# Three weight pieces under way instead of two, and a written order made again: attention with a top-128 expert layer on one core

## The chip, the core and the metric

The program runs on one core of a Trainium2 chip. The core has a matrix engine (TensorE, PE in the rows, with its weight loads as PEld), a vector engine (VectorE, DVE), a scalar engine (ScalarE, ACT), a general engine (GpSimd, POOL) and a sequencer that only issues transfers (SyncE, SP). Transfers of all queues are carried out by 16 DMA engines. The metric is the device time of one execution in microseconds (us); lower is better.

## The reference, cut to what matters

```python
# q, k, v: 8 batches x 12 heads x 448 tokens x 64
scores = cap * tanh(q @ k.T / sqrt(64) / cap)          # per head, 448 x 448
attn   = exp(scores - max) / (sum(exp(scores - max)) + 1e-9)
x      = (attn @ v), heads side by side                # 8 x 448 x 768
# expert layer, batch by batch
s      = x @ w_gate                                    # 448 scores
top    = the 128 tokens of the largest s
h      = relu(x[top] @ w1)                             # 128 x 1024
out    = x;  out[top] += sigmoid(s[top]) * (h @ w2)    # 128 x 768
```

## The kernel before, in words

Attention is cut into 24 *doubles* (three for each of 8 batches; a double is four heads), and each double into 7 *steps* of 64 key tokens, 168 steps in all. A step has one score product on TensorE (`ps`, line 450), a tanh and an exp on ScalarE (lines 501 and 504), one value product on TensorE that accumulates into `acc` (line 458), and a running sum of the exponentials on VectorE (`e`, line 554). Once per double VectorE turns the accumulator (`xT`, line 571), which frees the one PSUM accumulator for the next double; it turns and reduces the sums (lines 579 and 583), normalises (`xn` or `room`, line 674) and weighs the result for the token scores (lines 698 and 704).

After the third double of a batch comes its expert work. VectorE adds the token scores (`quads`, line 734); TensorE folds them (line 743); the score row goes out and comes back through HBM (`line`, `row`, lines 762 and 766) for every batch but the first; VectorE ranks every token (line 771) and builds the selection (`sel`, line 810); TensorE picks the indices (line 819); GpSimd gathers the 128 rows (`xe`, line 840). Then follow 36 matmuls with `w1` and 48 with `w2` per batch (line 961; each weight is held as a high and a low part, `w1h`, `w1l`, `w2h`, `w2l`), and GpSimd adds the result back with a scatter (line 1048; halves at line 1038 for the last batch). There are two `xe` buffers, so the selection of batch b can be written only when the scatter of batch b-2 has landed.

The weights come in 14 pieces of 128 rows, 6 of `w1` and 8 of `w2`. Of each piece GpSimd loads the high part (line 404), VectorE writes its negative into the low part (line 407, "cast"), and GpSimd loads the piece again and adds it into the low part (line 410). All 28 loads stand in GpSimd's queue in a fixed order, and a low load waits there for its cast.

The order of the work on all five engines is written by a planner before the program is built. It plays through the tasks with a duration for each, with a time for each transfer, and with a table `WAY` of eleven rows by 24 entries, which shifts priorities by double or stretch (`visit` and `enough`: how long TensorE stays at expert matmuls; `cast`: the 14 casts; and so on). The planner's own numbers set only this order; on the chip each engine runs its list in order and waits on semaphores for its operands.

Of the kernel before, what the change touches and what calls it, by code (L numbers as in the profile page):

```python
# [18 lines left out]
P = 128  # L19
# [21 lines left out]
ROWED = (1, 2, 3, 4, 5, 6, 7)  # L41
TURNED = (1, 2, 3, 4, 5), (1, 2, 3, 4)
WAY = {
    "visit": (14000, 8500, 14000, 4500, 7500, 7500, 1500, 7500, 5500, 2000, 2000, 1500, 6500, 3500,
        2500, 4500, 4000, 1500, 11000, 6000, 2500, 11000, 2500, 12500),
    "enough": (2, 3, 5, 5, 5, 5, 3, 1, 1, 3, 5, 3, 2, 2, 3, 5, 3, 2, 2, 5, 2, 5, 4, 1),
    "wait": (0, 1, 0, 0, 1, 1, 1, 1, 0, 0, 0, 0, 0, 0, 1, 0, 0, 0, 1, 1, 1, 1, 1, 0),
    "eager": (0, 2, 0, 2, 2, 0, 0, 0, 0, 0, 0, 0, 0, 0, 0, 0, 0, 0, 0, 0, 0, 0, 0, 0),
    "lag": (2, 2, 2.5, 3, 4, 2.5, 2.5, 4, 4, 2, 4, 4, 4, 2.5, 3, 4, 2.5, 2.5, 2.5, 3, 4, 4, 4, 4),
    "ask": (8, 0, -12, 12, 12, 0, -8, 8, 0, -4, -8, 8, 12, -8, -12, -8, -12, 8, -4, 12, 4, -8, -12,  # L50
        0),
    "fin": (14, 14, -4, -4, -8, -8, 0, -4, 8, 0, -4, -8, -8, 8, -8, 4, 0, -4, -4, -4, 14, 4, 8, 14),
    "turn": (20, 20, 0, 20, 20, 28, 10, 20, 20, 20, 28, 0, 0, 0, 0, 0, 0, -10, -10, 10, 10, 10, 20,
        20),
    "reserve": (30000, 30000, 0, 10000, 80000, 38000, 70000, 10000, 70000, 46000, 0, 0, 46000,
        70000, 70000, 46000, 20000, 20000, 30000, 46000, 30000, 46000, 46000, 0),
    "sums": (0, 8, 0, 0, 0, -2, 0, -2, -2, -2, -2, 8, -4, 0, -4, 0, 0, 0, 0, 0, 2, 8, 8, 0),
    "cast": (0, -20, 0, 10, 10, 10, 10, 10, 20, 10, 10, 10, 10, 10, 20, 20, 20, 0, -30, 20, -10,
        -10, 10, -30),
}  # L60


# [22 lines left out]
class Plan:  # L85
# [6 lines left out]
    def add(self, *a, **k):  # L92
        t = Task(*a, **k)
        t.n = len(self.tasks)
        self.tasks.append(t)
        return t
# [288 lines left out]
def w_tile(K, shape, dt, tag, i, name):  # L385
    return K.work.tile(shape, dt, tag=f"{tag}{i}", name=name, bufs=1)


def weights(tc, K, w1, w2, first=None, lv=None):
    nc = tc.nc  # L390
    parts = [(nm, w, i, m) for nm, w, n, m in (("w1", w1, K.ND, K.F), ("w2", w2, K.NF, K.DM))
             for i in range(n)]
    K.weights = {"w1": [], "w2": []}
    def pace(t):
        nc.gpsimd.tensor_copy(K.pace, first.v[0:1, 0, 0, 0:1])

    paced = K.plan.add("POOL", 120, pace, [lv], prio=-30) if lv else None
    before = [paced, paced]
    for n, (nm, w, i, m) in enumerate(parts):
        hi, lo = K.wts[nm + "h"][:, i, :], K.wts[nm + "l"][:, i, :]  # L400
        rows = w[i * P:(i + 1) * P, :]

        def high(t, hi=hi, rows=rows):
            nc.gpsimd.dma_start(hi, rows)

        def less(t, hi=hi, lo=lo):
            nc.vector.tensor_scalar(lo, hi.bitcast(F32), -1.0, None, op0=ALU.mult)

        def low(t, lo=lo, rows=rows):
            nc.gpsimd.dma_start(lo, rows, accum_op=ALU.add)  # L410

        h = K.plan.add("POOL", 950, high, before[:1], prio=3 * n, load=(1, P * m * 4), lat=1200)
        v = K.plan.add("DVE", 0.56 * m, less, [h], prio=6 + 3 * n, seg=("cast", n, 1))
        l = K.plan.add("POOL", 950, low, [v], prio=6 + 3 * n, load=(1, P * m * 5), lat=2000)
        before = [before[1], l]
        K.weights[nm].append(l)


# [295 lines left out]
def add_two(nc, out, two, both, n):  # L714
    if both is not None:
        nc.vector.tensor_reduce(out, both[:, :, :n].rearrange("p r c -> p c r"), axis=AX.X, op=ALU.add)
        return
    nc.vector.tensor_copy(out, two[0][:, :n])
    nc.vector.tensor_tensor(out, out, two[1][:, :n], op=ALU.add)


def select_tasks(tc, K, b):
    nc = tc.nc
    add, S, NCH, DM, NG = K.plan.add, K.S, K.NCH, K.DM, K.NG
    NB = S // Q
    vals = K.vals[b % 2]
    score = vals[:, 1, :]
    p0 = (b + 1) * NG * K.NS + 5
    ask = ("ask", (b + 1) * NG - 1, 1)
    box = {}  # L730

    def total(t):
        part, quads = K.part[b], K.quads[b % 2]
        nc.vector.tensor_tensor(quads[:, :NB], part[:, 0, :], part[:, 1, :], op=ALU.add)
        for g in range(2, NG):
            nc.vector.tensor_tensor(quads[:, :NB], quads[:, :NB], part[:, g, :], op=ALU.add)

    def fold(t):
        box["pc"], box["all"] = K.two(t)
        for i in range(2):  # L740
            for r in range(2):
                for m in range(2):
                    nc.tensor.matmul(box["pc"][r][HALF[m], :NCH], lhsT=K.fold[HALF[r], i, :],
                                     rhs=K.quads[b % 2][HALF[r], 2 * m + i::4], start=(i == 0),
                                     stop=(i == 1))

    def by_token(t):
        add_two(nc, score, box["pc"], box["all"], NCH)

    def rows(t):  # L750
        box["pr"] = K.two(t)[0][0]
        for c in range(NCH):
            nc.tensor.transpose(box["pr"][:, c * P:(c + 1) * P],
                                score[:, c:c + 1].to_broadcast([P, P]), K.ident)

    def row_copy(t):
        box["row"] = w_tile(K, [P, P * NCH], F32, "row", t.got["row"], "row")
        nc.vector.tensor_copy(box["row"].rearrange("p (q c) -> p c q", c=NCH),
                              box["pr"].rearrange("p (c q) -> p c q", c=NCH))

    def out_scores(t):
        nc.sync.dma_start(K.line[b % 2].rearrange("(p c) -> p c", c=NCH), score)

    def in_row(t):
        box["row"] = w_tile(K, [P, P * NCH], F32, "row", t.got["row"], "row")
        nc.sync.dma_start(box["row"], K.line[b % 2].partition_broadcast(P))

    def rank(t, c):
        m = min(P, S - c * P)
        jk = w_tile(K, [P, P, NCH], BF16, "jk", 0, "jk")  # L770
        nc.vector.scalar_tensor_tensor(  # L771
            out=jk[:m], in0=box["row"][:m].rearrange("p (q c) -> p q c", c=NCH),
            scalar=score[:m, c:c + 1], in1=K.least[:m, :, NCH - 1 - c:2 * NCH - 1 - c],
            op0=ALU.subtract, op1=ALU.is_ge, accum_out=K.rk[:m, c:c + 1])

    to = add("DVE", 340, total, K.scored[b], prio=p0, seg=ask)
    where = "S" if b else "X"
    fo = add("PE", 230, fold, [to], prio=-50, take=(where,), mode="att", late=True)
    bt = add("DVE", 70 if b else 330, by_token, [fo, *K.picked.get(b - 2, ())], prio=p0, seg=ask,
             give=[(where, fo)])  # L780
    if b in ROWED:
        ro = add("SP", 0, out_scores, [bt], prio=p0 - 30, load=(1, P * NCH * 4), lat=1200)
        landed = add("NONE", 0, lambda t: None, [ro], prio=-100)
        rc = add("SP", 0, in_row, [landed], prio=p0 - 30, take=("row", "rk"), load=(1, P * S * 4), lat=1500)
    else:
        ro = add("PE", 450, rows, [bt], prio=p0, take=(where,), mode="full")
        rc = add("DVE", 1030, row_copy, [ro], prio=p0, seg=ask, take=("row", "rk"),
                 give=[(where, ro)])
    count = [add("DVE", 680, lambda t, c=c: rank(t, c), [rc], prio=p0 + 1, seg=ask)
             for c in range(NCH)]  # L790
    add("NONE", 0, lambda t: None, count, prio=-100, give=[("row", rc)])
    final, hot = None, []
    for s0 in range(0, K.C, P):
        oh, final = expert_tasks(tc, K, b, s0, min(P, K.C - s0), count, final, vals, p0)
        hot.append(oh)
    add("NONE", 0, lambda t: None, hot, prio=-100, give=[("rk", rc)])
# [314 lines left out]
def end_batch(tc, K, D):  # L1111
    if D.grp < K.NG - 1:
        return
    b = D.b
    select_tasks(tc, K, b)
    K.plan.add("NONE", 0, lambda t: None, [*K.stores[b], *K.scored[b]], prio=-100,
               give=[("xn", K.first_n[b])])
# [92 lines left out]
def slow_path(tc, K, w1, w2):  # L1210
    K.plan = Plan(SIZES)
    K.fast_now = False
    K.last_heavy = [None, None]
    K.xn, K.part, K.xn_slot, K.first_n, K.stores, K.scored, K.picked = {}, {}, {}, {}, {}, {}, {}
    K.weighed = {}
    load_consts(tc, K)
    load_gate(tc, K)
    weights(tc, K, w1, w2)
    K.plan.run_in_order()
    general_path(tc, K)  # L1220
# [68 lines left out]
```

## Time and profile before

| | us |
|---|---|
| median of 3 runs | 443.87 (442.96 to 444.3) |
| the profiled execution | 443.99 |
| its span, first to last instruction | 442.2 |
| TensorE busy | 425.6 (96%) |
| VectorE busy | 370.6 (84%) |
| ScalarE busy | 347.2 (79%) |
| GpSimd busy | 49.1 (11%) |

The span is read in stretches: up to about 62 us only attention of the first batch is there; then expert matmuls come between the attention steps; the last score product stands near 374 us, and after it come mostly expert matmuls. A busy TensorE is not TensorE at its peak, since matmuls overlap in the array and their ends are modelled; so distances between starts are used as prices.

### The profile page before, as it was taken

How to read it: one execution, taken by the hardware profiler on the slowest of the kernel's cores; microseconds unless marked ns; L12 is line 12 of the kernel's file. 1: busy time of each engine (PE TensorE's matmuls, PEld its weight loads, DVE VectorE, ACT ScalarE, POOL GpSimd, SP SyncE). 2: the span in 40 equal slices, each digit the busy share in tenths (PEclk: the TensorE clock that was granted, in tenths of full speed). 3: DMA queues.
4: the chain of work that ended last, by engine and by line, in shares of the span. 5: the costliest groups of instructions: out<-in, count | busy, mean ns of one | idle time of the engine just before them, and what ended most of it. 6: DMA issues, size and time to landing. Idle time of an engine off the chain costs nothing. (4 is left out here: it accounts for less than half of the span.)

```text
span 442.2 us, 9958 instructions
## 1 busy us (share of the span) xinstructions
PE 425.6 (96%) x4106; PEld 233.1 (53%) x4106; DVE 370.6 (84%) x515; ACT 347.2 (79%) x403; POOL 49.1 (11%) x56
## 2 busy tenths in 40 slices
PE   8999899899999999999999999999999999999994
PEld 2242233344444548447554445644459539597984
DVE  3579999999999998999988999999997799853111
ACT  6999999999999993898859998899996598131320
POOL 5023110402101002000100000001002001002011
PEclk9999999899999999999999999999999999999998
DMA  7699996699935954792666943566782750552121
GB/s 241 238 249 249 320 274 185 183 254 261 217 132 151 224 125 110 207 308 65 161 168 181 223 144 110 139 168 152 252 207 64 178 152 1 109 115 36 37 36 42
DMA packets 58839, 73.72 MB, mean 167 GB/s; under 512 B 19266, under 2 KB 43202, under 8 KB 58786
## 3 DMA queue, kind: packets, MB, share of 16 engines
q1 hardware_dynamic: 52546, 53.67, 42.4%
q0 software_dynamic: 5808, 18.88, 19.7%
q8 instruction: 34, 0.56, 0.5%
q10 hardware_dynamic: 432, 0.46, 0.4%
q14 instruction: 19, 0.16, 0.1%
HBM read 54.76 MB, written 18.23 MB: 165 GB/s over the span
## 5 line engine op out<-in xcount | busy, mean ns | idle before, releaser
L501 ACT ACTIVATE p<-ps,sc 128x896 f32<-128x896 f32 (+1 forms) x169 | 164.8, 1014 | 15.2 <-PE ps L450 14.9
L504 ACT ACTIVATE p<-p,capc 128x896 f32<-128x896 f32 x168 | 171.0, 1060 | 0.4
L450 PE MATMUL ps<-qk 64*64 64x448 f32 x1288 | 148.0, 545 | 2.7 <-ACT p L501 2.6
L458 PE MATMUL acc<-p,v 64*64 64x448 f32 x1288 | 147.7, 545 | 2.3 <-DVE xT L571 1.1
L554 DVE TENSOR_TENSOR e<-e,p 128x896 f32<-128x896 f32 x119 | 128.2, 1078 | 8.3 <-ACT p L504 6.7
L450 PEld LDWEIGHTS ps<-qk 64*64 64x64 f32 x1288 | 44.6, 132 | 76.3 <-ACT p L501 40.3
L458 PEld LDWEIGHTS acc<-p,v 64*64 64x64 f32 x1288 | 46.5, 134 | 67.7 <-issue 49.3
L1048 POOL DMA_INDIRECT out<-xe,idx x7 | 12.7, 1809 | 216.1 <-ACT xe L1030 182.1
L987 ACT ACTIVATE hs<-pb 128x512 f32<-128x512 f32 x16 | 9.6, 600 | 31.8 <-PE pb L961 31.8
L961 PE MATMUL pb<-w2h,hh 128*128 128x384 f32 x128 | 28.4, 343 | 0.0
L571 DVE STREAM_TRANSPOSE xT<-acc 128x896 f32<-128x896 f32 x24 | 26.4, 1098 | 2.3 <-PE acc L458 2.3
L554 DVE TENSOR_TENSOR e<-p 128x896 f32<-128x896 f32 x24 | 25.8, 1075 | 2.9 <-ACT p L504 2.9
L961 PE MATMUL pb<-w2h,hl 128*128 128x384 f32 x128 | 28.2, 338 | 0.0
L961 PE MATMUL pb<-w2l,hh 128*128 128x384 f32 x128 | 28.2, 338 | 0.0
L771 DVE SCALAR_TENSOR_TENSOR jk<-row,vals,least 128x512 bf16<-128x512 f32 (+1 forms) x32 | 23.9, 746 | 3.7 <-DMA row<-line 2.9
L961 PE MATMUL pb<-w1h,xh 128*128 128x512 f32 x96 | 26.0, 399 | 0.0
L704 DVE TENSOR_REDUCE part<-jk 128x14 f32<-128x896 f32 x24 | 25.8, 1074 | 0.1
L579 DVE STREAM_TRANSPOSE turned<-e 128x896 f32<-128x896 f32 x23 | 25.3, 1100 | 0.3
L961 PE MATMUL pb<-w1l,xh 128*128 128x512 f32 x96 | 25.3, 395 | 0.0
L961 PEld LDWEIGHTS pb<-w2h,hh 128*128 128x128 f32 x128 | 22.2, 188 | 5.9 <-issue 4.9
L961 PE MATMUL pb<-w1h,xl 128*128 128x512 f32 x96 | 25.0, 394 | 0.0
L583 DVE TENSOR_REDUCE T<-turned 128x28 f32<-128x896 f32 x23 | 24.6, 1069 | 0.1
(106 smaller groups left out, 360.3 us busy)
## 6 DMA issues: line engine op xcount, KB each, us to landing
qk<-in_qk SPq DMA_DIRECT2D x46, 448.0 KB, 5.2
v<-in_v SPq DMA_DIRECT2D x23, 448.0 KB, 5.1
out<-xn SPq DMA_DIRECT2D x16, 224.0 KB, 4.4
out<-room SPq DMA_DIRECT2D x16, 224.0 KB, 3.9
w1h<-in_moe_w POOLq DMA_DIRECT2D x6, 512.0 KB, 8.4
w1l<-in_moe_w POOLq DMA_DIRECT2D x6, 512.0 KB, 8.1
w2h<-in_moe_w POOLq DMA_DIRECT2D x8, 384.0 KB, 8.9
w2l<-in_moe_w POOLq DMA_DIRECT2D x8, 384.0 KB, 7.2
```

The costliest lines, as they stand in the source:

```text
L450: tc.nc.tensor.matmul(ps[HALF[r], j, c0:c1], lhsT=D.qk[r][HALF[j], at:at + HD], rhs=D.qk[r][HALF[j], 2 * HD + c0:2 * HD + c1], start=True, ...
L458: tc.nc.tensor.matmul(D.acc[HALF[j], r, :K.S], lhsT=D.v[HALF[r], s, j, :], rhs=D.P[s][HALF[r], j, :], start=(s == 0), stop=(s == K.NS - 1))
L501: nc.scalar.activation(D.P[s][:, :, c0:c1], box[c0][:, :, c0:c1], AF.Tanh, scale=K.sc)
L504: nc.scalar.activation(D.P[s], D.P[s], AF.Exp, scale=K.cap)
L554: nc.vector.tensor_tensor(box["E"], box["E"] if n else D.P[s0], D.P[s], op=ALU.add)
L571: nc.vector.transpose(D.xT, D.acc[:, :, :S])
L579: nc.vector.transpose(box["turned"], parts[0]())
L583: nc.vector.tensor_reduce(box["T"], box["turned"].rearrange("p j (b k) -> p j b k", k=Q), axis=AX.X, op=ALU.add)
L704: nc.vector.tensor_reduce(K.part[b][:, grp, :], box["jk"], axis=AX.X, op=ALU.add)
L771: nc.vector.scalar_tensor_tensor(out=jk[:m], in0=box["row"][:m].rearrange("p (q c) -> p q c", c=NCH), scalar=score[:m, c:c + 1], in1=K.lea ...
L961: nc.tensor.matmul(X["acc" + n_ops][:M, :ns[1]], lhsT=X[l][:, i, :M], rhs=K.wts[r][:, i, ns[2]], start=bool(start and n == 0), stop=(stop ...
L1048: nc.gpsimd.indirect_dma_start(out=K.out[b], out_offset=bass.IndirectOffsetOnAxis(ap=X["idx"][:M], axis=0), in_=X["xe"][:M], in_offset=Non ...
```

## The change

Three things change. In `weights`, the high load of a piece is made to follow the low load of the piece three before it, where it was two before. In the planner's transfer times, a high load is counted 2500 ns later than its bytes in place of 1200, a low load 3000 in place of 2000, the score row's way out 3000 in place of 1200 and its way back 2500 in place of 1500. And the table `WAY` is another one, so that the order on every engine is written anew. The instructions are the same ones, and as many of each.

```diff
-    "visit": (14000, 8500, 14000, 4500, 7500, 7500, 1500, 7500, 5500, 2000, 2000, 1500, 6500, 3500,
...
+    "visit": (8000, 1500, 4500, 2000, 3500, 1500, 6000, 12500, 7000, 5500, 5500, 4500, 11000, 2000,
...
-    before = [paced, paced]
+    before = [paced] * 3
...
-        h = K.plan.add("POOL", 950, high, before[:1], prio=3 * n, load=(1, P * m * 4), lat=1200)
+        h = K.plan.add("POOL", 950, high, before[:1], prio=3 * n, load=(1, P * m * 4), lat=2500)
         v = K.plan.add("DVE", 0.56 * m, less, [h], prio=6 + 3 * n, seg=("cast", n, 1))
-        l = K.plan.add("POOL", 950, low, [v], prio=6 + 3 * n, load=(1, P * m * 5), lat=2000)
-        before = [before[1], l]
+        l = K.plan.add("POOL", 950, low, [v], prio=6 + 3 * n, load=(1, P * m * 5), lat=3000)
+        before = [*before[1:], l]
...
-        ro = add("SP", 0, out_scores, [bt], prio=p0 - 30, load=(1, P * NCH * 4), lat=1200)
+        ro = add("SP", 0, out_scores, [bt], prio=p0 - 30, load=(1, P * NCH * 4), lat=3000)
         landed = add("NONE", 0, lambda t: None, [ro], prio=-100)
-        rc = add("SP", 0, in_row, [landed], prio=p0 - 30, take=("row", "rk"), load=(1, P * S * 4), lat=1500)
+        rc = add("SP", 0, in_row, [landed], prio=p0 - 30, take=("row", "rk"), load=(1, P * S * 4), lat=2500)
```

The lines of the changed kernel are one lower than those before (404 is 403 there). On GpSimd's queue, the loads of the first pieces before, in their order:

```order
17 L404 DMA w1h<-in_moe_w 128x1024 x2
18 L410 DMA w1l<-in_moe_w 128x1024
19 L404 DMA w1h<-in_moe_w 128x1024
20 L410 DMA w1l<-in_moe_w 128x1024
21 L404 DMA w1h<-in_moe_w 128x1024
22 L410 DMA w1l<-in_moe_w 128x1024
23 L404 DMA w1h<-in_moe_w 128x1024
```

The same queue after the change, from the first load on:

```order
17 L403 DMA w1h<-in_moe_w 128x1024 x3
18 L409 DMA w1l<-in_moe_w 128x1024 x2
19 L403 DMA w1h<-in_moe_w 128x1024
20 L409 DMA w1l<-in_moe_w 128x1024
21 L403 DMA w1h<-in_moe_w 128x1024 x2
22 L409 DMA w1l<-in_moe_w 128x1024
23 L403 DMA w2h<-in_moe_w 128x768
```

Three high loads go out ahead of the first low load, where there were two; the gather of batch 0 (line 840, 839 after) has 18 of the 28 weight loads ahead of it before and 24 after.

On TensorE, the last `w2` matmuls of batch 0 before stand behind the fold of batch 1 (`quads_118`), the pick of batch 1 and the fold of batch 2 (`quads_117`), with 82 score products and 77 value products ahead of them:

```order
148 L743 MATMUL two<-quads_117,fold 64x4 x8
149 L450 MATMUL ps<-qk 64x448 x8
150 L458 MATMUL acc<-p,v 64x448 x4
151 L961 MATMUL pb<-w2h,hh 128x384 x4
152 L961 MATMUL pb<-w2l,hh 128x384 x4
153 L961 MATMUL pb<-w2h,hl 128x384 x4
154 L961 MATMUL pb<-w2h,hh 128x384 x4
155 L961 MATMUL pb<-w2l,hh 128x384 x4
156 L961 MATMUL pb<-w2h,hl 128x384 x4
157 L961 MATMUL pb<-w1h,xh 128x512 x6
```

After the change they stand next to the fold of batch 1, with 63 score products and 58 value products ahead:

```order
109 L742 MATMUL two<-quads_118,fold 64x4 x8
110 L457 MATMUL acc<-p,v 64x448 x4
111 L449 MATMUL ps<-qk 64x448 x4
112 L457 MATMUL acc<-p,v 64x448 x4
113 L600 MATMUL two<-T,same 64x14 x4
114 L960 MATMUL pb<-w2h,hh 128x384 x4
115 L960 MATMUL pb<-w2l,hh 128x384 x4
116 L960 MATMUL pb<-w2h,hl 128x384 x4
```

The whole expert work of batch 0 has moved ahead by 19 steps of attention, and the `w1` matmuls of batch 1 that followed it directly now come 22 score products after it.

Near the end of TensorE's list, the pick of the last batch (`vals_112`) before stands among the `w1` matmuls of batch 6:

```order
434 L961 MATMUL pb<-w1h,xh 128x512 x4
435 L867 MATMUL pb<-ident,hs 128x128 x4
436 L961 MATMUL pb<-w1h,xh 128x512 x2
437 L961 MATMUL pb<-w1l,xh 128x512 x3
438 L819 MATMUL two<-vals_112,sel 64x2 x16
439 L961 MATMUL pb<-w1l,xh 128x512 x3
440 L961 MATMUL pb<-w1h,xl 128x512 x6
```

After the change it stands here:

```order
422 L866 MATMUL pb<-ident,hs 128x128 x4
423 L960 MATMUL pb<-w1h,xh 128x512 x2
424 L960 MATMUL pb<-w1l,xh 128x512 x6
425 L960 MATMUL pb<-w1h,xl 128x512 x4
426 L818 MATMUL two<-vals_112,sel 64x2 x16
427 L960 MATMUL pb<-w1h,xl 128x512 x2
428 L960 MATMUL pb<-w2h,hh 128x384 x4
```

It is seven `w1` matmuls later; the matmuls around it are the same.

## Rows read from the trace of the kernel before

**Rows 1.** The page, busy time (share of the span) and instructions of three engines.
```profile
PE 425.6 (96%) x4106; PEld 233.1 (53%) x4106; DVE 370.6 (84%) x515; ACT 347.2 (79%) x403; POOL 49.1 (11%) x56
```

**Rows 2.** Windows: stretch, length, busy time of each engine, clock, DMA share, GB/s.
```profile
62.00:188.00 126.00, 121.72 (x1246) 59.94 (x1242) 122.62 (x174) 111.89 (x130) 15.84 (x16) 0.99 0.73 190
188.00:374.00 186.00, 184.82 (x1797) 102.66 (x1794) 174.50 (x223) 164.47 (x187) 8.76 (x6) 1.00 0.59 159
374.00:437.00 63.00, 61.01 (x437) 51.18 (x435) 25.16 (x49) 13.03 (x24) 7.72 (x6) 1.00 0.33 62
```

**Rows 3.** Waits of VectorE from 62 to 188 us: total, times, longest.
```profile
DVE sel L810 <- DMA out<-xe,idx: 1.7, 1, 1.7
DVE rec L615 <- PE two L601: 0.8, 2, 0.5
```

**Rows 4.** Timeline of VectorE: start, duration, instruction, [idle before, releaser].
```profile
62.35 1.11 DVE L571 STREAM_TRANSPOSE xT<-acc 128x896 f32<-128x896 f32 x1
63.38 1.05 DVE L554 TENSOR_TENSOR e<-e,p 128x896 f32<-128x896 f32 x1
...
175.49 0.69 DVE L810 SCALAR_TENSOR_TENSOR sel<-iota,rk 128x512 f32<-128x512 f32 x1 [1.68 <-DMA out<-xe,idx]
...
187.74 1.11 DVE L571 STREAM_TRANSPOSE xT<-acc 128x896 f32<-128x896 f32 x1
...
202.03 1.07 DVE L571 STREAM_TRANSPOSE xT<-acc 128x896 f32<-128x896 f32 x1
```

**Rows 5.** Timeline of TensorE: the last expert matmuls of batch 0, first of batch 1.
```profile
167.06 0.86 PE L961 MATMUL pb<-w2h,hl 128*128 128x384 f32 x4
167.76 1.54 PE L961 MATMUL pb<-w1h,xh 128*128 128x512 f32 x6
169.13 1.53 PE L961 MATMUL pb<-w1l,xh 128*128 128x512 f32 x6
```

**Rows 6.** Timeline of TensorE: attention, first value products of doubles 13 and 14.
```profile
186.61 0.93 PE L458 MATMUL acc<-p,v 64*64 64x448 f32 x8
187.36 0.93 PE L450 MATMUL ps<-qk 64*64 64x448 f32 x8
...
188.90 0.98 PE L458 MATMUL acc<-p,v 64*64 64x448 f32 x8
...
208.94 1.71 PE L458 MATMUL acc<-p,v 64*64 64x448 f32 x16
```

**Rows 7.** Timeline of GpSimd: weight loads, and the scatter of batch 0.
```profile
42.55 0.87 POOL L404 DMA_DIRECT2D w2h<-in_moe_w  x1
...
53.34 0.86 POOL L404 DMA_DIRECT2D w2h<-in_moe_w  x1
...
115.43 0.88 POOL L410 DMA_DIRECT2D w2l<-in_moe_w  x1 [4.18 <-DVE w2l L407]
...
168.82 2.40 POOL L1048 DMA_INDIRECT out<-xe,idx  x1 [34.02 <-DMA row<-line]
```

**Rows 8.** Timeline of TensorE: the pick of the last batch.
```profile
406.55 0.64 PE L819 MATMUL two<-vals,sel 64*64 64x2 f32 x32 [0.94 <-DVE sel L810]
```

**Rows 9.** Waits of TensorE from 188 us to the end: total, times, longest.
```profile
PE two L819 <- DVE sel L810: 1.4, 2, 0.9
PE two L601 <- ACT p L501: 0.5, 1, 0.5
PE two L601 <- DVE T L583: 0.4, 1, 0.4
PE acc L458 <- DVE xT L571: 0.4, 1, 0.4
```

**Rows 10.** DMA issues from 44 to 66 us: size each, median us to landing.
```profile
w2h<-in_moe_w POOLq DMA_DIRECT2D x2, 384.0 KB, 10.4
w2l<-in_moe_w POOLq DMA_DIRECT2D x2, 384.0 KB, 9.0
w1l<-in_moe_w POOLq DMA_DIRECT2D x1, 512.0 KB, 8.3
```

**Rows 11.** Windows as in Rows 2, early stretches.
```profile
9.00:24.00 15.00, 14.59 (x188) 4.62 (x184) 6.93 (x8) 15.00 (x17) 4.09 (x6) 1.00 0.70 237
24.00:44.00 20.00, 19.38 (x252) 7.18 (x248) 19.16 (x28) 20.00 (x23) 4.30 (x7) 1.00 1.01 262
44.00:66.00 22.00, 19.46 (x208) 6.58 (x204) 21.86 (x29) 21.41 (x24) 3.31 (x5) 1.00 1.08 296
66.00:88.00 22.00, 19.48 (x212) 6.90 (x210) 21.74 (x36) 20.31 (x24) 5.79 (x7) 0.92 0.64 188
```

**Rows 12.** Timeline of TensorE: its longest wait.
```profile
80.14 1.64 PE L450 MATMUL ps<-qk 64*64 64x448 f32 x8 [1.77 <-ACT p L501]
```

More of the change, by code (lines that the diff above doesn't have):

```diff
@@ L43 @@
 WAY = {
-    "visit": (14000, 8500, 14000, 4500, 7500, 7500, 1500, 7500, 5500, 2000, 2000, 1500, 6500, 3500,
[L45 to L56, printed above, removed]
@@ L57 @@
-    "sums": (0, 8, 0, 0, 0, -2, 0, -2, -2, -2, -2, 8, -4, 0, -4, 0, 0, 0, 0, 0, 2, 8, 8, 0),
-    "cast": (0, -20, 0, 10, 10, 10, 10, 10, 20, 10, 10, 10, 10, 10, 20, 20, 20, 0, -30, 20, -10,
-        -10, 10, -30),
+    "visit": (8000, 1500, 4500, 2000, 3500, 1500, 6000, 12500, 7000, 5500, 5500, 4500, 11000, 2000,
+        8000, 6000, 3000, 14000, 14000, 14000, 8500, 4000, 6500, 5500),
+    "enough": (5, 3, 2, 5, 2, 3, 1, 3, 4, 2, 4, 4, 4, 1, 4, 1, 1, 1, 1, 5, 1, 4, 1, 1),
+    "wait": (1, 1, 0, 1, 1, 1, 0, 0, 1, 1, 1, 0, 0, 1, 0, 1, 0, 1, 1, 0, 1, 0, 0, 1),
@@ new lines @@
+    "eager": (0, 2, 2, 2, 2, 0, 0, 0, 1, 1, 2, 0, 0, 0, 0, 0, 0, 0, 0, 0, 0, 0, 0, 0),
+    "lag": (1, 1, 1.5, 2, 2, 2.5, 2.5, 4, 4, 4, 4, 4, 2, 4, 2, 2, 4, 4, 4, 4, 4, 4, 4, 4),
+    "ask": (12, -12, 0, 12, 0, 12, 8, 8, 8, -4, 0, 12, 12, -12, -12, -4, -4, 8, 8, 8, 4, 4, 4, 4),
+    "fin": (-8, 0, 4, 8, -8, 4, -8, 14, 8, -4, 0, -4, 8, 4, -8, -8, 4, 0, 0, -8, 14, -4, 14, 4),
+    "turn": (20, 10, -10, 28, 28, 28, -10, 20, 0, 0, 0, 20, 10, 10, 0, 28, 20, 28, 10, 20, -10, 10,
+        28, 28),
+    "reserve": (20000, 50000, 50000, 50000, 50000, 20000, 20000, 20000, 50000, 30000, 54000, 42000,
+        30000, 0, 80000, 54000, 30000, 0, 20000, 38000, 30000, 20000, 20000, 10000),
@@ L60 @@
+    "sums": (8, -4, 2, 2, 2, 2, 2, 0, -2, -2, -2, -2, -2, 8, 4, -2, 0, 0, 0, 0, 0, -2, 0, 8),
+    "cast": (10, 20, 10, 20, 20, 20, 20, 20, 10, -30, -20, -30, -30, -20, -30, -20, -30, 20, -20,
+        -20, 0, -20, -10, 0),
 }
```

## The prediction, on record before the result was known

> **What bounds the kernel now.** I read the page's busy times first [rows 1], then the windows by stretch [rows 2], then the waits, then the timelines. The page says TensorE, at 96%, but that share is an average over stretches, so I asked the windows which engine has no room left in each. From 62 to 188 us VectorE works 122.6 of 126.0 us, and nearly all that is missing are two kinds of waits: 1.7 us for the selection of batch 2, which stands until the scatter of batch 0 has landed, and 0.8 us for sums of TensorE [rows 2, 3]. TensorE in the same stretch is shown busy 121.7 us, but its parts are stretched: four matmuls of attention (eight records) take 0.75 us from start to start [rows 6], which makes 1.5 us for a step, and VectorE needs more than that for a step and its share of the rest. The place where the one hands the time to the other is the accumulator: at 187.74 us VectorE starts to turn the accumulator of double 12, and the first value product of double 13 starts at 188.90, 1.16 us later, which is the 1.11 us of the turn and its signal [rows 4, 6]. So up to 188 us the pace is VectorE's. From 188 to 374 us TensorE works 184.8 of 186.0 us, and after 374 us 61.0 of 63.0 [rows 2]; there the pace is TensorE's, and whatever does not shorten its list or its waits is worth nothing.
>
> **The change part by part.** No instruction is added or removed, so only idle time on the pacing engine can come or go. I counted both written orders up to the same point, the turn of double 12 and the first value product of double 13.
>
> Ahead of that value product TensorE has in both kernels the same list: 700 score and value matmuls (175 products of four), 72 of `w1`, 48 of `w2`, three picks, three folds. Ahead of that turn VectorE has in both 137 large operations of about 1.0 us (62.35 to 63.38 for one [rows 4]), 12 rankings, 14 casts, three selections and the same expert splits; after the change one reciprocal more, which I count at 0.3 us. Equal lists end at a different time only through waits. VectorE's early part is also the same: ahead of the turn that starts at 62.35 us there are 38 large operations in both, and one cast more after, so there is no head start.
>
> The 1.7 us wait goes. Before, the last `w2` matmuls of batch 0 end at 167.8 us, just before the first `w1` matmuls of batch 1, its scatter is issued at 168.82, and the selection of batch 2 starts at 175.49 [rows 4, 5, 7]. After the change those `w2` matmuls stand 19 steps of attention earlier; 38 products of 0.75 us are 28.6 us. The scatter's landing then comes near 147 us and cannot be what the selection of batch 2 waits for. The 0.8 us for sums I leave, since nothing shows it gone. First term: 1.7 - 0.3 = 1.4 us earlier at the first value product of double 13. Bounds: at the good end all 2.5 us of [rows 3] go; at the bad end the early casts cost VectorE waits of their own (the rival below), so this term reaches from -2.5 to +4.4.
>
> Does the 1.4 us last? For double 14, VectorE has 5.2 us more ahead of its turn than before (four large operations and one `xt`), while TensorE's list is the same again. Before, the product came 208.94 - 202.03 - 1.11 = 5.8 us after the turn was done [rows 4, 6]. The turn is now 5.2 later in VectorE's list, and 1.4 us of lead are common to both, so 0.6 us of cover stay, and with it the lead. If that cover were short by a microsecond, the lead would shrink by as much.
>
> From there TensorE's list holds the same instructions in both kernels, and the count of changes between attention and expert matmuls is 27 in both, so I move nothing there, except one wait that I can see. The pick of the last batch stands 0.94 us for its selection [rows 8], which itself waits for the scatter of batch 5. In the new order seven more `w1` matmuls stand ahead of it; six take 1.37 us (167.76 to 169.13 [rows 5]), so seven take 1.6 us, more than the wait. Second term: 0.9 us. The other waits of TensorE in this part, 2.7 - 0.9 = 1.8 us in all [rows 9], are the bound below; above, one new wait of the longest kind seen, 1.77 us [rows 12].
>
> The planner's longer transfer times change only the order. The score rows' way is one of them: its ranking is not a wait in [rows 3], so I give it nothing.
>
> Three pieces under way: the casts of the last pieces move up in VectorE's list by some 24 us of its work, so the last low load, at 115.43 us before [rows 7], would go out near 91 us. TensorE first needs `w2` near 110 us in the new order, and all of it near 124, so with landings of 9 to 10 us [rows 10] TensorE does not wait for weights. VectorE might: a cast waits in line for its high load and holds back everything behind it, sums and turns included. I followed GpSimd's list against the casts: the shortest time from issue to cast is about 10 us, for the second piece of `w2`, issued near 44.5 and cast near 54.5. Before, the pair at 42.55 and 53.34 us had 11 to 12 us, and landings took 10.4 us [rows 7, 10]. It is close; but by 51 us the new order has put out no more than one transfer beyond the old one, and that one early, between 9 and 24 us, where the DMA engines are busy 0.70 of the time [rows 11]. I take zero, and price the failure below.
>
> One rule speaks against the third piece. From 24 to 66 us the DMA engines are busy 1.01 and 1.08 of the time [rows 11]. The Trainium skill (DMA: Bandwidth & Descriptors, Issuing engines are not separate DMA queues) says that transfers of all queues run on the same 16 engines and interleave. By it a third piece in that stretch only lengthens every landing, the pieces come no sooner, and the waits go to VectorE. The same page (Anatomy of one DMA, SWDGE path) puts one such load at 2.0 us plus its bytes over 436 GB/s, an estimate of 2.9 us for 384 KB; the rows show 10.4 us under this load, so the measured number decides, and by the page's number the first rule's rival would fall away.
>
> **Sum.** 443.99 (profiled execution; span 442.2 and 1.8 around it) - 1.4 - 0.9 = 441.7 us. That execution is 0.12 us above the median of 443.87, which I neglect. What this kernel's measurement can tell from no change is about 0.3%, 1.3 us, so "faster" begins at 442.5.
>
> **Rivals.** *Slower: casts wait for late loads.* Place: VectorE between 50 and 90 us, where its time is the kernel's. By 56 us the new order has three transfers more under way than the old. From 44 to 66 us the DMA engines were already full, so each costs its place in line, and I price one at 1.5 us (384 KB at the 296 GB/s of [rows 11], 1.3 us, and something for the second read of the adding load): 4.4 us. Then 441.7 + 4.4 = 446.1 us. It decides as soon as the second `w2` piece takes over 10.0 us to land; for it speak the 10.4 of [rows 10], against it the nearly equal number of transfers by 51 us.
>
> *No change: the lead is given back.* The lead of 1.4 us reaches the stretch paced by TensorE, and the new places of expert work bring as many new waits (a pick, a sum or a turn that is late by a microsecond, as in [rows 9]). A wait there may cost twice: around the 1.77 us wait [rows 12] the granted clock is 0.92 over 22 us [rows 11], which is some 1.8 us at the lower of its two levels. Before, VectorE's pace hid that; after 188 us nothing would. Result 443.5 to 444.3, 443.9.
>
> *Faster by more.* The other waits of 1.8 us and 0.8 us go too: 441.7 - 2.6 = 439.1 us. For it: the planner now counts transfers nearer to what the rows show. Against it: those waits have nothing to do with transfers.
>
> **Chances.** Forecast 0.42 (its own range 440.4 to 442.8), more gain 0.15, no change 0.22, slower 0.21. Faster takes nearly all of the first and the second, 0.55; same 0.23; slower 0.22. The range for 8 in 10 runs from 438.8 to 446.0, which leaves out the far ends of the second and the last case.
>
> **What would show it.** In the profile after: the scatter of batch 0 near 135 to 147 us and no wait of the selection of batch 2; the first value product of double 13 near 187.5 us; VectorE without waits for `w1h` or `w2h` between 40 and 90 us; the last low load near 91 us; no wait at the pick of the last batch. I am wrong if casts stand for loads, if the turn of double 14 paces the product, or if TensorE's waits after 188 us are clearly over 2.7 us.

## The result, and the profile after

The changed kernel takes 448.86 us (median of 4 runs, 447.85 to 450.05) against 443.87: a ratio of 1.0116, 95% interval 1.0086 to 1.0147. It is slower by 1.2%, 5.0 us, where I had said 2.2 us faster. Lines of the kernel after have numbers one lower from the list of weights on (the cast is L406, the loads L403 and L409, the selection L809). Pieces of weights are numbered 0 to 13 here; 0 to 5 are `w1`, 6 to 13 `w2`.

The page of the profiled execution (449.21 us, span 447.4), busy times as in [rows 1]:

```profile
PE 427.3 (96%) x4106; PEld 234.9 (53%) x4106; DVE 370.7 (83%) x515; ACT 349.3 (78%) x403; POOL 48.4 (11%) x56
```

VectorE's sum hardly differs; TensorE's is 1.7 us and ScalarE's 2.1 us longer with the same number of instructions. Most of the 5 us must lie in waits, and the windows say in which stretch. Columns as in [rows 2]:

```profile
44.00:66.00 22.00, 20.23 (x212) 6.28 (x206) 21.72 (x29) 22.00 (x25) 5.01 (x7) 1.00 1.06 298
66.00:88.00 22.00, 17.88 (x180) 7.46 (x178) 16.66 (x30) 16.09 (x19) 6.27 (x8) 0.84 1.01 258
62.00:188.00 126.00, 118.49 (x1198) 59.99 (x1202) 117.60 (x164) 108.15 (x125) 10.71 (x12) 0.97 0.69 180
188.00:374.00 186.00, 184.07 (x1808) 101.17 (x1801) 172.28 (x224) 163.78 (x184) 10.31 (x7) 1.00 0.62 165
```

From 62 to 188 us VectorE works 117.6 us in place of 122.6 [rows 2], and nearly all of those 5.0 us are missing between 66 and 88 us: 16.66 in place of 21.74 [rows 11]. There the clock column says 0.84 and the DMA engines are busy all the time (1.01, before 0.64). VectorE's waits from 62 to 188 us name it, in the columns of [rows 3]:

```profile
DVE w2l L406 <- DMA w2h<-in_moe_w: 4.5, 2, 3.3
DVE e L553 <- ACT p L503: 1.4, 1, 1.4
DVE rec L614 <- PE two L600: 0.8, 1, 0.8
DVE xT L570 <- PE acc L457: 0.6, 1, 0.6
```

VectorE's timeline shows the place: the casts of pieces 9 and 10 stand amid the ranks of batch 0, behind the copy of the score row, and the selection of batch 0 (75.82) needs all four ranks.

```profile
65.13 1.21 DVE L757 COPY row<-pb 128x512 f32<-128x512 f32 x1
69.61 0.56 DVE L406 TENSOR_SCALAR w2l<-w2h 128x768 fp32r<-128x768 f32 x1 [3.27 <-DMA w2h<-in_moe_w]
...
72.88 0.56 DVE L406 TENSOR_SCALAR w2l<-w2h 128x768 fp32r<-128x768 f32 x1 [1.24 <-DMA w2h<-in_moe_w]
...
75.82 0.68 DVE L809 SCALAR_TENSOR_TENSOR sel<-iota,rk 128x512 f32<-128x512 f32 x1
...
192.49 1.10 DVE L570 STREAM_TRANSPOSE xT<-acc 128x896 f32<-128x896 f32 x1
```

TensorE stands with it, for the selection of batch 0, and meets its value product of double 13 at 193.65 us in place of 188.90 [rows 6]:

```profile
76.55 1.03 PE L818 MATMUL pb<-vals,sel 64*64 64x2 f32 x32 [4.12 <-DVE sel L809]
...
193.65 2.49 PE L457 MATMUL acc<-p,v 64*64 64x448 f32 x24
```

GpSimd's timeline shows why the loads are late. The load of piece 9 is the one issued at 52.55 us, that of piece 10 the one at 55.24; six loads go out between 50.53 and 55.24, where before there were four from 52.79 to 55.80.

```profile
43.49 0.87 POOL L403 DMA_DIRECT2D w2h<-in_moe_w  x1
50.53 1.25 POOL L409 DMA_DIRECT2D w1l<-in_moe_w  x1 [6.17 <-DVE w1l L406]
51.09 1.24 POOL L403 DMA_DIRECT2D w2h<-in_moe_w  x1
51.99 1.23 POOL L409 DMA_DIRECT2D w2l<-in_moe_w  x1
52.55 1.22 POOL L403 DMA_DIRECT2D w2h<-in_moe_w  x1
54.69 0.86 POOL L409 DMA_DIRECT2D w2l<-in_moe_w  x1 [0.92 <-DVE rec L617]
55.24 0.85 POOL L403 DMA_DIRECT2D w2h<-in_moe_w  x1
...
95.45 0.85 POOL L409 DMA_DIRECT2D w2l<-in_moe_w  x1 [2.80 <-DVE w2l L406]
140.71 1.60 POOL L1047 DMA_INDIRECT out<-xe,idx  x1 [44.41 <-DMA out<-xn]
```

And the high loads in the window from 44 to 66 us, with the median time to landing, against the 10.4 us of [rows 10] (the load at 43.49 reaches into the window and is counted; it took 10.3 us, those of pieces 9 and 10 took 17.0 and 17.6):

```profile
w2h<-in_moe_w POOLq DMA_DIRECT2D x4, 384.0 KB, 17.0
```

The engines moved 298 GB/s there, before 296 [rows 11]: more loads under way, no more bytes, longer landings. VectorE reached the cast of piece 9 at 66.3 us, 13.8 us after its load was issued; with the old landing of 10.4 us it would not have waited. Issued earlier, the piece did land earlier than before, at 69.6 us (52.55 + 17.0) in place of 74.4 (66.09 + 8.3). But the new order had moved its cast up by more: before, that cast ran at 85.23 us, behind the selection of batch 0.

**The account at the first value product of double 13.** Waits of VectorE after: 4.5 + 1.4 + 0.8 + 0.6 = 7.3 us. Before: 1.7 + 0.8 = 2.5 [rows 3]. The difference, 4.8 us, agrees with the shift of that product (193.65 - 188.90 = 4.75). Of the 5.2 us between the two profiled executions 0.45 is left for all that follows.

### The profile page after: what moved, and what is told of

Same layout as the page of the kernel before. It is cut to its first block, busy times and chain, and to the rows that moved or that the text cites. A ratio compares the mean times of both kernels' runs of the same rounds, so it can differ in the third digit from the quotient of the medians.

```text
span 447.4 us, 9949 instructions
## 1 busy us (share of the span) xinstructions
PE 427.3 (96%) x4106; PEld 234.9 (53%) x4106; DVE 370.7 (83%) x515; ACT 349.3 (78%) x403; POOL 48.4 (11%) x56
## 5 line engine op out<-in xcount | busy, mean ns | idle before, releaser
L500 ACT ACTIVATE p<-ps,sc 128x896 f32<-128x896 f32 (+1 forms) x169 | 164.3, 1017 | 12.5 <-PE ps L449 10.3
L449 PEld LDWEIGHTS ps<-qk 64*64 64x64 f32 x1288 | 47.2, 134 | 75.9 <-ACT p L500 33.4
L1029 ACT ACTIVATE xe<-pb,both 128x384 f32<-128x384 f32 x14 | 8.1, 580 | 24.7 <-PE pb L960 24.7
## 6 DMA issues: line engine op xcount, KB each, us to landing
w1h<-in_moe_w POOLq DMA_DIRECT2D x6, 512.0 KB, 10.4
```

The lines of the kernel that those rows point to most:

```text
L449: tc.nc.tensor.matmul(ps[HALF[r], j, c0:c1], lhsT=D.qk[r][HALF[j], at:at + HD], rhs=D.qk[r][HALF[j], 2 * HD + c0:2 * HD + c1], start=True, ...
L500: nc.scalar.activation(D.P[s][:, :, c0:c1], box[c0][:, :, c0:c1], AF.Tanh, scale=K.sc)
```

## The experiments

The order edits below work on the finished order that the planner hands out, a list of tasks from which each engine takes its own in turn. `later(order, tasks, anchor, engine, count)` moves tasks behind an anchor and `count` more tasks of an engine (VectorE if none is named).

**late_casts: the waiting casts out of the ranks.**

```
+    later(order, [("l", 8), ("h", 11)], ("cast", 8))
+    later(order, [("cast", 9), ("l", 9), ("h", 12)], ("h", 11), count=2)
+    later(order, [("cast", 10), ("l", 10), ("h", 13)], ("h", 12), count=2)
+    (casts and low loads 11 and 12 change places)
```

> The kernel after, with one edit: the casts of weight pieces 9 and 10 (the second and third piece of w2 counted from 8, the ones for which VectorE stood 3.27 and 1.24 us amid the ranks of batch 0) stand behind the selection of batch 0, and the casts of pieces 8 to 13 are in the order of their loads; all else of the written order is the same, three pieces stay under way. Theory (the casts that stand for late loads are the loss): the waits of 4.5 us are gone, the selection of batch 0 starts near 71.3 us in place of 75.82, the turn of double 12 near 188 in place of 192.5, the time is about 444.4 (443.5 to 445.5). Rival (the new table's order is worse by itself, for instance by the visit of 36 w2 matmuls from 133 to 140 us, or TensorE paces that stretch): the waits go but the time stays at 447.5 or more.

Measured: 452.43 us, ratio 1.0172 (1.0135 to 1.0208), slower than the kernel after. The two waits were gone and the selection of batch 0 started at 70.83 us, as expected (one later cast stood 1.8 us for its load, at 82.40 us). But my edit made a new and longer wait. First GpSimd's timeline around the gather of batch 0, then the gather's landing, then what TensorE waited for:

```profile
73.28 0.87 POOL L437 DMA_DIRECT2D w2l<-in_moe_w  x1 [16.87 <-DVE w2l L434]
...
77.23 0.87 POOL L431 DMA_DIRECT2D w2h<-in_moe_w  x1
78.42 1.04 POOL L868 DMA_INDIRECT xe<-out,idx  x1 [0.32 <-issue]
```

```profile
xe<-out,idx POOLq DMA_INDIRECT x1, 13.4
```

```profile
PE pb L896 <- ACT xp L958: 5.8, 1, 5.8
```

Six loads from 73.28 to 77.23 us stand ahead of the gather (the expectation of the next run counts five); it landed after 13.4 us (7.4 us in the kernel before), and TensorE, with ScalarE and VectorE behind it, stood 5.8 us for the gathered rows. The run does not tell the theories apart, but it shows the same loss with another consumer: work written ahead of the landing that it needs.

**casts_past_gather: the same, with the gather first.**

```
+    later(order, [("cast", 8), ("l", 8), ("h", 11)], ("gather", 0))
+    later(order, [("cast", 9), ("l", 9), ("h", 12)], ("h", 11), count=2)
+    later(order, [("cast", 10), ("l", 10), ("h", 13)], ("h", 12), count=2)
+    later(order, [("cast", 11), ("l", 11)], ("h", 13), count=9)
+    (casts and low loads 12 and 13 behind that, three tasks apart)
```

> The kernel after; the casts of weight pieces 8 to 13, in the order of their loads, with their low loads and the high loads 11 to 13, stand behind the gather of batch 0 on GpSimd's queue and behind its index on VectorE. In the run late_casts the 4.5 us wait for w2h was gone too, but five weight loads were issued from 73.28 to 77.23 us, just ahead of the gather, which took 13.4 us to land, and TensorE then stood 5.8 us for the gathered rows. Here the gather goes first. Theory (what costs is a consumer written ahead of its load's landing: first the casts, then the gather): no wait for w2h, the gather lands in 8 us or less, the turn of double 12 starts near 187.5 us, the time is 443.7 (443.0 to 444.7). Rival (the new table's order is worse by itself): 447 or more without those waits.

Measured: 444.8 us, ratio 1.0024 (1.0007 to 1.0041). VectorE's waits from 40 to 190 us, the gather's landing, and the turn of double 12:

```profile
DVE e L586 <- ACT p L536: 1.4, 1, 1.4
DVE both L750 <- PE pb L851: 0.8, 1, 0.8
DVE rec L647 <- PE two L633: 0.8, 1, 0.8
DVE w2l L438 <- DMA w2h<-in_moe_w: 0.5, 1, 0.5
```

```profile
xe<-out,idx POOLq DMA_INDIRECT x1, 5.1
```

```profile
189.05 1.10 DVE L603 STREAM_TRANSPOSE xT<-acc 128x896 f32<-128x896 f32 x1
```

The edit moves the casts and low loads of pieces 8 to 13 and the high loads of 11 to 13, and nothing else. With the rest of the new order untouched, the ratio falls from 1.0116 to 1.0024: 4.1 us of the 5.0 are back. The turn is 1.3 us behind the 187.74 of [rows 4] in place of 4.75. The rival (the new order is worse by itself) wanted 447 or more; it keeps about the last 1.1 us (0.3 to 1.8 by the interval). The four waits that are left add up to 3.5 us, 1.0 more than the 2.5 before, which is most of the 1.3 us at the turn; no run here takes them away alone. The cast that still waits is that of piece 7, the second piece of `w2`, whose load took 10.7 us here:

```profile
54.35 0.56 DVE L438 TENSOR_SCALAR w2l<-w2h 128x768 fp32r<-128x768 f32 x1 [0.51 <-DMA w2h<-in_moe_w]
```

**stall_before: the same stand put into the kernel before.**

```
+    def stall(t):
+        for _ in range(7):
+            K.nc.vector.tensor_scalar(K.hs, K.wts["w1h"][:, 0, :].bitcast(F32), -1.0, None, op0=ALU.mult)
+    order.insert(place(order, ("sel", 0)), (Task("DVE", 4500, stall), {}))
```

> The kernel before, with seven more VectorE operations on a buffer that nothing uses then (a cast-like copy of 128x1024, about 0.62 us each, 4.3 us together) just ahead of the selection of batch 0. Theory (VectorE paces this stretch, so what it stands there for is lost at the end one to one): 443.9 + 4.3 = 448.2 us, perhaps 0.5 to 1 us more from a lower granted clock of TensorE behind it. Rival (there is slack in that stretch, or the loss after has another source): 443.9 to 445.5.

Measured: 448.66 us, ratio 1.0105 (1.0074 to 1.0136). The page and TensorE's longest wait of it, then the window 66 to 88 us:

```profile
PE 425.9 (95%) x4106; PEld 234.0 (52%) x4106; DVE 375.4 (84%) x522; ACT 347.0 (78%) x403; POOL 49.6 (11%) x56
```

```profile
PE pb L847 <- DVE sel L838: 5.0, 1, 5.0
```

```profile
66.00:88.00 22.00, 16.17 (x180) 6.26 (x176) 21.54 (x36) 16.29 (x20) 2.23 (x3) 0.84 0.49 150
```

VectorE's busy time grew by 4.8 us (375.4 - 370.6), its waits fell from 2.5 us to 1.9, and the kernel grew by 4.5 (448.66 against 444.13 for the kernel before beside it; 4.1 between the two profiled executions). So VectorE is the pace there, nearly one to one, and a stand of this size alone gives the kernel after its time. TensorE stood 5.0 us and its granted clock fell here as it did after (0.84 in that window), and the sum needs nothing for it: a lower clock on an engine that does not set the pace did not show in the time.

**third_held: one load fewer in the bunch.**

```
+    later(order, [("h", 10)], ("l", 9))
+    later(order, [("cast", 10), ("l", 10)], ("h", 13), count=1)
```

> The kernel after; the high load of weight piece 10, the last of the six loads issued from 50.5 to 55.2 us, is held back behind the cast of piece 9 (issued near 70 us), and its cast stands later too, behind high load 13. So in that stretch one transfer fewer is under way, issued after the load of piece 9 that VectorE stands for. Theory A (transfers under way share the DMA engines, whichever was issued first): piece 9 lands 1.5 to 2 us earlier, its cast waits 1.3 to 1.8 us in place of 3.27, the cast of piece 10 no longer waits: 448.9 - 1.2 - 1.7 = 446.0 us. Theory B (the transfers of one queue land in the order of issue, what is issued later does not matter): the cast of piece 9 still waits 3.0 us or more: 447.6 us.

Measured: 447.33 us, ratio 1.0094 (1.0057 to 1.0131), which can't be told from the kernel after. The load of piece 9, now issued at 53.02 us, and its cast:

```profile
53.02 1.24 POOL L426 DMA_DIRECT2D w2h<-in_moe_w  x1
```

```profile
71.01 0.56 DVE L429 TENSOR_SCALAR w2l<-w2h 128x768 fp32r<-128x768 f32 x1 [4.50 <-DMA w2h<-in_moe_w]
```

By its numbers this is theory B: 18 us from issue to cast, though one of the two loads behind it was gone (the low load of piece 7 still went out at 54.94). One trace can't settle the 1.5 to 2 us that theory A asked for: with the same loads ahead, that load took 17.0 us to land in the kernel after, 18.0 here and 15.7 in casts_past_gather. So it was not seen to gain, and no more. What every trace shows is the order: none of the loads that GpSimd issued landed ahead of one issued before it. Here the bunch from 51.00 to 54.94 us lands at 64.5, 66.6, 69.6, 71.0 and 73.1 us, and piece 9 is the fourth in that line. How much of its 18 us is due to the loads ahead of it and how much to the other queue, no run here parts. The cast of piece 10 no longer waited, but the total wait stayed at 4.5 us.

**no_low_567: less traffic ahead.**

```
-            nc.gpsimd.dma_start(lo, rows, accum_op=ALU.add)
+            if n not in (5, 6, 7):
+                nc.gpsimd.dma_start(lo, rows, accum_op=ALU.add)
```

> The kernel after, without the adding loads of the low parts of weight pieces 5, 6 and 7 (their part of the result is left out); every other instruction and the order are the same. Theory (the high loads land late because the pieces under way share the DMA engines): the median landing of the w2 high loads between 44 and 66 us falls from 17.0 to 10 us or less, no cast waits, the time is 444 to 445. Rival (the landing is long for another reason, such as the stores of batch 0 on the other queue): landings stay above 14 us and the casts still wait.

Measured: 443.24 us, ratio 0.9983 (0.9958 to 1.0007), and no wait for `w2h`. Its high loads from 44 to 66 us:

```profile
w2h<-in_moe_w POOLq DMA_DIRECT2D x4, 384.0 KB, 11.1
```

The waits are gone, as the theory had it; the landing, 11.1 us, is just over the 10 it named, and the time just under its 444 to 445. But by leaving out three loads the run changes two things: GpSimd no longer stood for the casts ahead of those low loads, so the high loads 8 to 10 went out at 44.3 to 45.3 us, some 7 to 10 us earlier. Shorter landing and earlier issue can't be parted in it.

**before_no_scatter: the prediction's first term alone.**

```
     def scatter(t):
+        if b == 0:
+            return
```

> The kernel before, without the scatter of batch 0 (its part of the result is left out), so that the selection of batch 2 has no transfer to wait for: the 1.68 us wait that the prediction's first term counted as a gain. The prediction's view: 443.9 - 1.4 = 442.5 us. Rival: the wait stands inside TensorE's visit of 36 w1 matmuls that ends at 176.1 us, and VectorE's next operation is a reciprocal of sums that TensorE makes right behind that visit, so VectorE waits for TensorE until 176.5 us instead: the first value product of double 13 stays at 188.9 us and the time within 0.4 us of 443.9.

Measured: 443.41 us, ratio 0.9990 (0.9975 to 1.0005): no gain that can be told from none, and by the interval at most 1.1 us of the 1.4. VectorE's timeline, to be held against the selection in [rows 4]:

```profile
173.30 0.68 DVE L810 SCALAR_TENSOR_TENSOR sel<-iota,rk 128x512 f32<-128x512 f32 x1
176.07 0.52 DVE L615 RECIPROCAL rec<-two 128x28 f32<-128x28 f32 x2 [2.09 <-PE two L601]
```

The selection starts 2.2 us earlier and the next operation waits 2.09 us for sums that TensorE makes only behind its 36 `w1` matmuls. The wait has changed its name.

**before_sums_first: that wait taken away too.**

```
+    held = [("mm", 1, "11", True, n) for n in range(18)] + [("relu", 1, 1)]
+    later(order, held, ("mm", 1, "10", True, 17), "PE", 3)
+    (selection of batch 2 three VectorE tasks later; the weighing and its sum right behind it)
```

> The kernel before; TensorE's last 18 w1 matmuls of batch 1 stand behind the two sums and the value product that follow them, and VectorE's selection of batch 2 stands behind the reciprocals and the normalising that follow it (the weighing and its sum stand ahead of the use of the pick). So neither the scatter of batch 0 nor TensorE's long visit holds VectorE from 173.7 to 176.9 us. Theory (VectorE's idle time there is the kernel's if all its causes go together): the first value product of double 13 starts near 187.4 in place of 188.9 us and the time is 442.2 to 442.6. Rival (another wait takes its place, or TensorE's stretch behind 188 us gives the lead back): 443.5 or more.

Measured: 444.61 us, ratio 1.0023 (1.0007 to 1.0039). The sums came at 171.93 us, and VectorE waited further on, for ScalarE, whose scores TensorE makes only behind the same matmuls:

```profile
181.79 1.09 DVE L589 TENSOR_TENSOR e<-e,p 128x896 f32<-128x896 f32 x1 [1.84 <-ACT p L539]
```

Three different releasers in three kernels (the scatter in the kernel before, TensorE's sums, ScalarE), and 1.7 to 2.1 us each time: the stand goes with TensorE's visit of expert matmuls, whatever VectorE waits for in name. My theory of it (VectorE's idle time there can be had) fell.

**w2_apart and w2_pairs: the long visit of the new order cut up.** Both add to casts_past_gather:

```
+    for part, behind, count in ((False, ("21", True), 12), (True, ("20", False), 6)):    # w2_pairs: 4 and 2
+        held = [("mm", 0, "21", part, n) for n in range(12)]
+        held += [] if part else [("gated", 0, 1), ("scatter", 0)]
+        later(order, held, ("mm", 0, *behind, 11), "PE", count)
```

> As casts_past_gather, and the 36 w2 matmuls of batch 0 that TensorE does in one visit of 6.3 us (133.29 to 139.74 in the kernel after) are three visits of 12, with six products of attention between them; the gating of the second half and the scatter of batch 0 move along. Theory (that visit starves ScalarE and, through it, VectorE, which stood 1.41 us for p and 0.75 us for sums at 142 to 145 us): 2 us less than casts_past_gather, about 441.7, which would be faster than both kernels. Rival (VectorE's stand there is made up for later, or the added changes of TensorE between attention and expert work cost as much): within 0.7 us of casts_past_gather.

> As casts_past_gather, and the 36 w2 matmuls of batch 0 are three visits of 12 with one score product and one value product between them, and the sums of the softmax stay behind all 36 (in w2_apart these sums had come ahead of their operand: TensorE stood 3.7 us for it, and VectorE then 5.0 us for the accumulator). In casts_past_gather ScalarE stood 3.58 us from 132.8 to 136.4 us for that visit, and VectorE behind it 0.75 and 1.41 us. Theory (those stands of VectorE are lost time): 1.4 to 2.2 us less than casts_past_gather, that is 442.6 to 443.4. Rival (made up for later): 444.5 to 445.

Measured: 450.23 us, ratio 1.0159 (1.0130 to 1.0188), and 445.82 us, ratio 1.0047 (1.0027 to 1.0068). Neither gained. In w2_apart the sums stood ahead of their operand in TensorE's line (first its wait, then VectorE's), and in w2_pairs both of VectorE's waits grew, from 0.75 and 1.41 us:

```profile
PE two L637 <- DVE T L619: 4.5, 2, 3.7
```

```profile
DVE xT L607 <- PE acc L494: 5.0, 1, 5.0
```

```profile
DVE e L590 <- ACT p L540: 2.0, 1, 2.0
DVE rec L651 <- PE two L637: 1.5, 1, 1.5
```

**three_old_table and table_two_pieces: the parts of the change alone.** The first has the old table of numbers with three pieces and the new landings, the second the new table and landings with `[paced] * 2`.

> The kernel after with the table of numbers of the kernel before: three pieces under way and the later landings in the planner, but the old table, so the planner writes another order; in it the casts of pieces 9 to 13 stand behind the selection of batch 0. Theory (only a cast placed ahead of its load's landing costs): no wait for w2h amid the ranks, 443 to 445.5 us. Rival (three pieces under way cost by themselves, by DMA engines that are full): 446.5 us or more, with waits for weights elsewhere or longer operations.

> The kernel after with two pieces of weights under way in place of three: new table and new landings, so the planner writes another order; the casts of pieces 7 to 13 stand behind the selection of batch 0 there. Theory (the loss hangs on the third piece and where it puts the casts): no cast waits for w2h over 1 us, the landings of w2h between 44 and 66 us are near 10 us; the time is 443 to 447, because the table was made for another count of pieces. Rival (the table is worse by itself): 447 or more, without any such wait.

Measured: 458.51 us, ratio 1.0309 (1.0271 to 1.0346), and 453.87 us, ratio 1.0224 (1.0189 to 1.0259). By their numbers both fall on the rivals' side, by their place they don't. From 40 to 190 us no cast waits more than 0.4 us in either. The high loads of three_old_table from 44 to 66 us, then TensorE's stretch from 188 to 374 us in three_old_table and in table_two_pieces:

```profile
w2h<-in_moe_w POOLq DMA_DIRECT2D x4, 384.0 KB, 10.4
```

```profile
188.00:374.00 186.00, 178.39 (x1751) 96.82 (x1751) 164.58 (x211) 155.53 (x177) 9.58 (x6) 1.00 0.60 160
```

```profile
188.00:374.00 186.00, 179.94 (x1752) 100.84 (x1744) 163.25 (x209) 150.50 (x172) 11.82 (x8) 1.00 0.59 159
```

TensorE misses 6 to 8 us there, before 1.2 [rows 2]: each run gives the planner another order, and both orders are bad. That is about half of what the two lose (14.4 and 10.3 us against the kernel before beside them); the rest is not followed here. So the parts can't be priced one by one: three_old_table sets the old table against the new count and the new transfer times at once. It says one thing more: with three pieces under way and the loads further apart (four from 52.58 to 55.60 us, as before) the landing stays at 10.4 us, so the count alone does not lengthen it.

## Why the prediction was wrong

**The step that failed first: the cost of the casts, taken as zero.** I held the time from issue to cast, at its shortest 10 us for the second piece of `w2`, against the landing of before, 10.4 us. That piece, issued at 43.49 us, landed after 10.3 us, just as its cast came up (53.83 us). The pieces that were late are the fourth and fifth of `w2` (9 and 10), whose casts came up 13.8 and 16.4 us after their issue. I counted transfers only up to 51 us and used the old landing for all that came behind, while it went up to 17.0 and 17.6 us. The new order is one load ahead up to 50.53 us and two just behind that; at 52.55 us, when the load of piece 9 goes out, it is five ahead (17 loads against 12), and by 56 us the three that my rival named. The prediction moved the casts up by some 24 us and did not ask by how much their loads would come sooner: 4.8 us for piece 9, while VectorE came to its cast 18.9 us sooner (66.3 in place of 85.23).

**The slower rival was the right case, and its price came out in part by luck.** Its place and its cause held: VectorE between 50 and 90 us, casts that stand for late loads. Its price, 4.4 us, is close to the 4.5 us measured, but not by its working, which took three transfers of 1.5 us each as the delay of a load without slack. The load of piece 9 took 6.6 us longer to land than the old 10.4; its cast had 3.4 us of slack (13.8 - 10.4), which leaves its wait of 3.3, and the other 1.2 us are those of a second cast. Its deciding point, over 10.0 us for the second piece, was met by a hair and decided nothing: 10.3 us without a wait here, 10.7 us with a wait of 0.5 in casts_past_gather. Its total, 446.1 us, stood on the forecast's 2.3 us of lead, which did not come. Without that lead it is 443.99 + 4.4 = 448.4 us, against the 449.21 of the profiled execution.

**The first term, 1.4 us, was not there.** The step itself came true: the scatter of batch 0 is issued at 140.71 us, and the selection of batch 2 waits for nothing. But taking the wait away gained nothing in the kernel before (before_no_scatter: 0.9990): it lay beside TensorE's visit, and the sums behind that visit were next. The new order has such a stand at another place, 0.75 + 1.41 us behind the 36 `w2` matmuls from 133.29 to 139.74 us. I had read VectorE's share of 97% as its pace over the whole stretch; in the few microseconds of such a visit it is TensorE that paces.

**The second term, 0.9 us, did not show in the time.** The pick of the last batch no longer waits, and another wait of that size stands in TensorE's stretch, as the no-change rival had it:

```profile
321.08 0.98 PE L449 MATMUL ps<-qk 64*64 64x448 f32 x8 [1.09 <-DVE rec L614]
...
412.89 0.64 PE L818 MATMUL two<-vals,sel 64*64 64x2 f32 x32
```

All waits of TensorE from 188 us to the end, in the columns of [rows 9]:

```profile
PE ps L449 <- DVE rec L614: 1.1, 1, 1.1
PE two L818 <- DVE sel L809: 0.9, 2, 0.5
PE two L600 <- DVE T L582: 0.3, 1, 0.3
```

They add up to 2.3 us in place of 2.7, yet from the first value product of double 13 to the end the kernel after takes 0.45 us longer; where that lies is not shown. The no-change rival also put a lower clock at 1.8 us: that is what 0.92 over 22 us takes away, and the time at the lower level is twice as long. In stall_before, with 0.84 over the same stretch, it cost nothing that showed.

**The signs I had named.** Right: the scatter, the selection of batch 2, the last pick, and TensorE's waits after 188 us, which stayed under 2.7 us; the last low load at 95.45 us is the 91 I had said and the 4.5 us of the casts. The turn ahead of double 14 did not pace its product, though only 0.14 us were left (it ends at 213.12 us, the product starts at 213.26) where I had counted 0.6. Wrong: the value product (193.65, not 187.5) and the waits for `w2h`. What stays open is the last 1.1 us of casts_past_gather, and which of the loads and queues made the landing longer.

## What to carry to other kernels

An instruction that waits in line for a transfer must be held against the landing under the new traffic at its own place, not against the landing of before: here, with the DMA engines full, loads issued in a closer bunch moved no more bytes and landed later, and a consumer moved up by 19 us met a load that came 5 us sooner. A wait in the profile is worth its length only if the next instruction on that engine has its operands by then; look at what is queued behind it before counting it as a gain. And here the planner's table went with its rules: with one of the two changed alone the order was worse than either kernel's, so the parts couldn't be tried one by one.

## What was not expected of the hardware

- Three pieces under way moved 298 GB/s from 44 to 66 us, two moved 296; the median landing of a 384 KB load went from 10.4 to 17.0 us. With three under way but the loads further apart it was 10.4 (three_old_table). The Trainium skill (DMA: Bandwidth & Descriptors, Issuing engines are not separate DMA queues) says that all queues share the same 16 engines; the trace agrees, at a DMA share of 1.06: 0.54 is that of the queue with the weight loads and 0.52 that of the queue with the loads and stores of attention.
- In every trace, the loads of GpSimd's queue landed in the order of their issue. A load was not seen to gain from holding back the one issued after it (18.0 us to its landing in third_held, 17.0 in the kernel after, but 15.7 in casts_past_gather with nothing held).
- The gather of batch 0 landed after 5.1 us with the weight loads behind it (casts_past_gather) and after 13.4 us with six of them issued in the 5.1 us ahead (late_casts).
